# A fused attention, feed-forward and routed-expert kernel: weights converted in pairs, three step tables, smaller fixed expert capacities

## Chip, cores, metric

One core of a Trainium2 chip. The time is the device time of one execution in microseconds (us); the median of the runs is quoted. All inputs are in DRAM at the start, the output is in DRAM at the end.

## What is computed

Three layers in a row, cut from the reference:

```python
scores = scale * np.matmul(q, k.transpose(0, 1, 3, 2))        # B, H, S, D = 4, 8, 576, 64
kth = np.partition(scores, -32, axis=-1)[..., -32:-31]
scores = np.where(scores >= kth, scores, -1e9)                # the 32 largest of a row stay
x = (softmax(scores) @ v)  ->  [2304, 512]
h = x @ w_in; g = h * np.clip(h + 3, 0, 6) / 6; x = g @ w_out # w_in 512x2048, w_out 2048x512, float64
expert_idx = np.argmax(xn @ en.T / tau, axis=1)               # 8 second experts, one of them per token
out[mask] = gate_w[mask, None] * (np.maximum(x[mask] @ w1[e], 0) @ w2[e])   # w1 512x1024, w2 1024x512
```

`w_in` and `w_out` come as float64 and are taken apart on the chip; `w1` and `w2` are float32. Every float32 product is made of three TensorE products of a high and a low part (fp32r).

## The kernel before

**The step loop.** The attention is cut into 72 units (a head pair by 128 queries). `step(i)` runs in a loop of 76 steps and issues, for unit i and the four before it, one short operation after the other: scores (`score`), copies from PSUM (`take`), the selection of the 32 largest on VectorE (`pairs`, L409 to L413, and `pick0` to `pick3`, L428 and L431), the bounds on GpSimd (`bounds`, L436), relu and exp on ScalarE (`bend`, `expo`), a subtraction on GpSimd (`mask`, L446), transposes (`turn`, `keep`) and the product with v (`values`). From step 12 on a step also issues one eighth of a group of 256 tokens of the feed-forward layer (`s10`, `s11`, `gate`, `swish`, `large`, `small`, `s20`, `s21`). The order inside a step is a string of names: `FIRST` in steps 0 to 20, `THEN` afterwards. The engines run their own instructions in just that order, so each engine's queue is written out by hand here.

**Taking the weights apart.** In steps 0 to 18 the steps also convert `w_in` and `w_out`: 32 pairs of pieces of 128 x 256 values, one pair a step in steps 0 to 4 and two from step 5 on. A piece of float64 arrives as two int32 words each. VectorE makes the float32 bits of it with two scalar_tensor_tensor instructions (`w_one`, L234; `w_two`, L238), each over 128 x 256 and each with two tensors in SBUF. For three pieces of four ScalarE makes the rounding (`w_round`, L246) and GpSimd adds it (`w_add`, L251); for the fourth VectorE adds the next bits instead (L241). `w_hi` (ScalarE, L259) and `w_low` (GpSimd, L263) then split a pair into high and low part, and the low part goes to DRAM (`lo_dram`).

**After the loop** the rest of the feed-forward layer is issued through a scheduler (`whole`), eight parts per group. Each group of 128 tokens is routed: transposes, a product with the expert embeddings, `choose` (five small VectorE instructions), `rank` (two products and four small VectorE instructions) and `place` (an indirect DMA on GpSimd that writes a token's number into a table in DRAM). The last two groups are treated apart, in a part with an order written out (`tc.manual_schedule`): their transposes and routing stand between pieces of `stage1(0, 0, 256, ...)`, the first product of the first expert, and `split2(0, ...)` (ScalarE copy and VectorE subtraction of that expert's `w2`, L806 and L807) comes after `rank`.

**The second experts** are taken in the order of their token counts. Expert of rank r works on a fixed number `CAPS[r]` of tokens, gathered with indirect DMAs in blocks of up to 128 (`tokens`, L822, L826). `stage1` is 96 matmuls with `CAPS[r]` columns (L964), `stage2` 24 matmuls of 512 columns per block (L977). Rank 5 has a second bound: a conditional block behind all others (`tc.If(more > 0)`) takes tokens 256 to 383 when there are any. A block for whatever is above the capacities (`over_`) stands behind that.

Of the kernel before, what the change touches and what calls it, by code (L numbers as in the profile page):

```python
# [54 lines left out]
def fused_kernel(tc: tile.TileContext, *args):  # L55
# [35 lines left out]
def layers(tc: tile.TileContext, qt, kt, v, w_in, w_out, embt, tau, w1, w2, out, y_dram, g_dram, x_dram, tbl, lo_dram, flag, pools, consts):  # L91
# [4 lines left out]
    m1, sm, fs, ps_a = pools[1:]  # L96
# [15 lines left out]
    ordi = const.tile([1, 2 * E + 2], I32, name="ordi")  # L112
# [10 lines left out]
    stg = st.enter_context(tc.tile_pool(name="stg", bufs=5))  # L123
# [24 lines left out]
    def embed(part):  # L148
# [6 lines left out]
        elif part == 1:  # L155
            onesf = mp.tile([128, 128], F32, tag="ug", name="onesf", bufs=1)
            nc.vector.memset(onesf, 1.0)
            sq = fs.tile([128, 4, E], F32, tag="gts", name="sq")
            nc.vector.tensor_tensor(sq, emb["et"], emb["et"], op=ALU.mult)
# [3 lines left out]
        elif part == 2:  # L163
# [45 lines left out]
    def w_load(n):  # L209
        raws = []  # L210
        for src, dst in (wpieces[2 * n], wpieces[2 * n + 1]):
            single = src.dtype == F32
            if single:
                raw = stg.tile([128, 256], F32, tag="st", name="w32")
                nc.sync.dma_start(out=raw, in_=src)
            else:
                raw = stg.tile([128, 256, 2], I32, tag="st", name="w64")
                nc.sync.dma_start(out=raw, in_=src.bitcast(I32).rearrange("p (n two) -> p n two", two=2))
                cnt[0] += 1
            raws.append((raw, single, cnt[0] % 4 != 3))  # L220
        ent_[n] = dict(dst=wpieces[2 * n][1], raws=raws)

    def words_of(e):
        return [(raw, e["both"][:, 256 * o:256 * o + 256].bitcast(I32), rounded)
                for o, (raw, single, rounded) in enumerate(e["raws"]) if not single]

    def w_one(n):
        e = ent_[n]
        e["both"] = mp.tile([128, DM], F32, tag="wf", name="wf", bufs=3)
        for o, (raw, single, _) in enumerate(e["raws"]):  # L230
            if single:
                nc.vector.tensor_copy(e["both"][:, 256 * o:256 * o + 256], raw)
        for raw, t, _ in words_of(e):
            nc.vector.scalar_tensor_tensor(t, raw[:, :, 1], 3, raw[:, :, 1], op0=ALU.logical_shift_left, op1=ALU.bitwise_xor)  # L234

    def w_two(n):
        for raw, t, _ in words_of(ent_[n]):
            nc.vector.scalar_tensor_tensor(t, t, 0x3FFFFFFF, raw[:, :, 1], op0=ALU.bitwise_and, op1=ALU.bitwise_xor)  # L238
        for raw, t, rounded in words_of(ent_[n]):
            if not rounded:  # L240
                nc.vector.scalar_tensor_tensor(t, raw[:, :, 0], 29, t, op0=ALU.logical_shift_right, op1=ALU.bitwise_or)  # L241

    def w_round(n):
        for raw, single, rounded in ent_[n]["raws"]:
            if rounded and not single:
                nc.scalar.activation(raw[:, :, 0], raw[:, :, 0].bitcast(U32), AF.Copy, scale=2.0 ** -29)  # L246

    def w_add(n):
        for raw, t, rounded in words_of(ent_[n]):
            if rounded:  # L250
# [919 lines left out]
```

## Time and profile before

| | |
|---|---|
| median of 3 runs | 1165.76 us (1165.2 to 1168.55) |
| the profiled execution | 1164.9 us, its span 1163.2 us |
| busy, share of the span | TensorE 87%, weight loads 77%, VectorE 70%, ScalarE 63%, GpSimd 56% |
| mean granted TensorE clock | 0.937 |

Busy shares are means over stages with different limits, so the kernel is read by stretches: the step loop with the conversion (0 to about 241 us), the step loop without it (to about 748 us), the rest of the feed-forward layer (to about 885 us) and the second experts. A row of the view by lines gives source line, engine, operation, tiles and shape, then the group's busy time, the mean duration of one in ns, and the idle time of the engine before them with what ended it.

### The profile page before, as it was taken

To read this page: it belongs to the slowest core of one execution; us is meant where nothing else is said; L and a number is where in the kernel's file an instruction comes from. 1 tells how busy PE (TensorE), PEld (TensorE's weight loads), DVE (VectorE), ACT (ScalarE), POOL (GpSimd) and SP (SyncE) were. 2 spreads that over 40 slices of the span, in tenths; PEclk is the share of its full clock that TensorE was granted. 3 is DMA by queue.
4 is the path that set the end of the run, shared out by engine and by line. 5 is a ranking of instruction groups with operands and counts; after the bars stand their busy time and mean duration, and the time that the engine had idled before them with its cause. 6 is when DMAs were issued, how large, how long until landed. Compare 5 with 4: busy or idle time off the path is not lost. (4 is left out here: it accounts for less than half of the span.)

```text
span 1163.2 us, 21146 instructions
## 1 busy us (share of the span) xinstructions
PE 1008.5 (87%) x7200; PEld 892.1 (77%) x7200; DVE 818.5 (70%) x2429; ACT 732.6 (63%) x1486; POOL 646.4 (56%) x833
## 2 busy tenths in 40 slices
PE   2455576789999979999979998999989999999994
PEld 1344465679998869998868997889978788888884
DVE  4999999999788968788968789922142534444440
ACT  4676776878778868778868778743334444444540
POOL 5676776777666867666867666653231442213210
PEclk9966577889999989999989999999999999999998
DMA  6444455665443446443446244356765463344440
GB/s 179 146 137 138 164 167 174 185 199 204 123 123 116 134 144 194 123 123 118 136 121 213 82 146 128 110 128 177 235 214 208 117 221 122 128 175 148 173 175 20
DMA packets 93014, 176.45 MB, mean 152 GB/s; under 512 B 21135, under 2 KB 38690, under 8 KB 92895
## 3 DMA queue, kind: packets, MB, share of 16 engines
q1 hardware_dynamic: 88255, 164.90, 45.2%
q0 software_dynamic: 4640, 10.10, 2.6%
q8 instruction: 59, 0.97, 0.4%
q14 instruction: 60, 0.49, 0.1%
HBM read 151.15 MB, written 19.71 MB: 147 GB/s over the span
## 5 line engine op out<-in xcount | busy, mean ns | idle before, releaser
L446 POOL TENSOR_TENSOR s<-s,z 128x576 f32<-128x576 f32 x144 | 189.8, 1323 | 70.2 <-ACT z L442 69.5
L568 PE MATMUL bank_h<-xh,vh 128*128 128x256 f32 x576 | 177.0, 307 | 0.8 <-DVE u L580 0.8
L568 PE MATMUL bank_h<-xh,lo 128*128 128x256 f32 x576 | 167.7, 291 | 3.7 <-DMA lo<-lo_dram 3.7
L568 PE MATMUL bank_h<-xl,vh 128*128 128x256 f32 x576 | 167.7, 291 | 2.8 <-DVE xl L524 2.8
L428 DVE MAX8 A<-left 128x8 f32<-128x288 f32 (+1 forms) x288 | 159.7, 595 | 0.0
L397 PE MATMUL ps_sc<-kst,qh 128*128 128x288 f32 x256 | 90.8, 367 | 71.6 <-DVE left L413 35.9
L587 POOL TENSOR_TENSOR gl<-u,gh 128x512 fp32r<-128x512 f32 x72 | 93.2, 1295 | 102.8 <-ACT gh L584 88.8
L484 ACT COPY pt<-bank_t 128x384 f32<-128x384 f32 x216 | 100.4, 475 | 59.1 <-PE bank_t L479 58.9
L479 PE MATMUL bank_t<-ident,s 128*128 128x128 f32 x648 | 108.2, 294 | 28.0 <-ACT pt L484 16.7
L397 PEld LDWEIGHTS ps_sc<-kst,qh 128*128 128x128 f32 x256 | 55.7, 218 | 88.4 <-issue 73.6
L400 ACT COPY s<-ps_sc 128x576 f32<-128x576 f32 x144 | 91.5, 635 | 41.8 <-PE ps_sc L397 38.4
L568 PEld LDWEIGHTS bank_h<-xh,lo 128*128 128x128 f32 x576 | 114.2, 198 | 4.3 <-DMA lo<-lo_dram 4.3
L568 PEld LDWEIGHTS bank_h<-xl,vh 128*128 128x128 f32 x576 | 114.3, 198 | 3.6 <-DVE xl L524 3.1
L580 DVE SCALAR_TENSOR_TENSOR u<-u,bank_h 128x512 f32<-128x512 f32 x72 | 49.2, 684 | 95.6 <-ACT u L576 95.3
L603 PE MATMUL y<-wh,gh 128*128 128x512 f32 x288 | 116.3, 404 | 0.0
L807 DVE TENSOR_TENSOR l<-a,h 128x1024 fp32r<-128x1024 f32 x64 | 78.0, 1243 | 54.2 <-ACT h L806 51.5
L479 PEld LDWEIGHTS bank_t<-ident,s 128*128 128x128 f32 x648 | 82.3, 150 | 44.0 <-ACT pt L484 20.1
L568 PEld LDWEIGHTS bank_h<-xh,vh 128*128 128x128 f32 x576 | 114.2, 198 | 1.6 <-DVE u L580 1.0
L603 PE MATMUL y<-wh,gl 128*128 128x512 f32 x288 | 113.0, 397 | 2.0 <-POOL gl L587 2.0
L603 PE MATMUL y<-lo,gh 128*128 128x512 f32 x288 | 113.9, 396 | 0.2 <-DMA lo<-lo_dram 0.2
L442 ACT ACTIVATE z<-s,nb 128x576 bf16<-128x576 f32 x144 | 111.7, 780 | 0.8 <-POOL nb L436 0.7
L452 ACT ACTIVATE s<-s,nb 128x576 f32<-128x576 f32 x144 | 112.1, 778 | 0.0
(240 smaller groups left out, 2778.9 us busy)
## 6 DMA issues: line engine op xcount, KB each, us to landing
lo<-lo_dram SPq DMA_DIRECT2D x144, 512.0 KB, 4.2
a<-in_moe_w_dram SPq DMA_DIRECT2D x64, 512.0 KB, 7.4
qraw<-in_q_dram SPq DMA_DIRECT2D x64, 128.0 KB, 3.0
w<-in_moe_w_in_dram SPq DMA_DIRECT2D x32, 256.0 KB, 3.4
lo_dram<-wf SPq DMA_DIRECT2D x32, 256.0 KB, 2.4
w<-in_moe_w_out_dram SPq DMA_DIRECT2D x32, 256.0 KB, 3.0
vt<-in_v_dram SPq DMA_DIRECT2D x16, 320.0 KB, 4.5
kraw<-in_k_dram SPq DMA_DIRECT2D x32, 144.0 KB, 4.3
```

Of the source, the lines that this page charges most:

```text
L397: nc.tensor.matmul(ps[:, n, :HS], t, kk[:, HS * g:HS * g + HS], start=(o == 0), stop=(o == len(parts) - 1))
L400: nc.scalar.copy(sbuf[i % NS][:, :, HS * g:HS * g + HS], ps_[i][:, :, :HS])
L428: nc.vector.max(A[:, n, 8 * r:8 * r + 8], src[:, n, :w])
L442: nc.scalar.activation(zb_[n], tile_of(i, n), AF.Relu, bias=sel[i][1][:, n, 1:2], scale=-BIG)
L446: nc.gpsimd.tensor_tensor(s, s, zb_[n], op=ALU.subtract)
L452: nc.scalar.activation(s, s, AF.Exp, bias=sel[i][1][:, n, 0:1], scale=SCALE, accum_out=sums[i][:, n:n + 1])
L479: nc.tensor.transpose(pp[:, 128 * k:128 * k + 128], e[:, 128 * (3 * c + k):128 * (3 * c + k) + 128], ident)
L484: nc.scalar.copy(pts[i][:, 3 * c:3 * c + 3, :].rearrange("p k n -> p (k n)"), tb_.pop((i, c))[:, :384])
L568: nc.tensor.matmul(ph[:, a, :], w, x[:, k, :], start=(k == 0 and n == 0), stop=(k == 3 and n == 2))
L587: nc.gpsimd.tensor_tensor(state[q][1], state.pop((q, "u")).rearrange("p (a n) -> p a n", a=2), state[q][0].bitcast(F32), op=ALU.subtract)
L603: nc.tensor.matmul(state["y"][o], x[:, a, c], w, start=(f == 0 and n == 0), stop=(f == 15 and n == 2))
L807: nc.vector.tensor_tensor(lo, x, hi.bitcast(F32), op=ALU.subtract)
```

## The change

- `w_load` reads a whole pair with one DMA into one tile of 128 x 512 double words, three of them in turn instead of five half as wide. `w_one` becomes one tensor_scalar over 128 x 512 (shift and mask with constants), `w_two` one scalar_tensor_tensor over 128 x 512, `w_round` and `w_add` one instruction each over 128 x 512, for all pairs; the instruction of L241 is no longer used.
- Three tables: `FIRST` in steps 0 to 11, `MID` in steps 12 to 20, `THEN` afterwards, all with new orders (they are left out below; the pieces that the prediction speaks of are shown as instructions).
- `embed`, which prepares the expert embeddings, goes in five parts instead of four; its squares move from VectorE to ScalarE and its matmul to the step after them.
- `CAPS` falls by 32 for ranks 1, 2 and 3 and by 48 for rank 4; the conditional block of rank 5 goes.
- The part with the order written out for the last two groups goes. They are routed like all others, and the scheduler places `stage1(0, 0, 256)` and `split2(0)`. The weights of the second expert are asked for after the tables of all experts, and the value of its number is loaded there too.

```diff
-CAPS = (480, 384, 352, 336, 304, 256, 256, 240)
+CAPS = (480, 352, 320, 304, 256, 256, 256, 240)
-LAST, MOST = 5, 384
...
     def w_one(n):
         e = ent_[n]
+        raw = e["raw"]
         e["both"] = mp.tile([128, DM], F32, tag="wf", name="wf", bufs=3)
...
-        for raw, t, _ in words_of(e):
-            nc.vector.scalar_tensor_tensor(t, raw[:, :, 1], 3, raw[:, :, 1], op0=ALU.logical_shift_left, op1=ALU.bitwise_xor)
+        nc.vector.tensor_scalar(t, raw[:, :, 1], 3, 0x3FFFFFFF, op0=ALU.logical_shift_left, op1=ALU.bitwise_and)
     def w_two(n):
-        for raw, t, _ in words_of(ent_[n]):
-            nc.vector.scalar_tensor_tensor(t, t, 0x3FFFFFFF, raw[:, :, 1], op0=ALU.bitwise_and, op1=ALU.bitwise_xor)
-        for raw, t, rounded in words_of(ent_[n]):
-            if not rounded:
-                nc.vector.scalar_tensor_tensor(t, raw[:, :, 0], 29, t, op0=ALU.logical_shift_right, op1=ALU.bitwise_or)
+        nc.vector.scalar_tensor_tensor(t, raw[:, :, 1], -0x40000000, t, op0=ALU.bitwise_and, op1=ALU.bitwise_or)
...
-        for name in (FIRST if i < WORDS else THEN).split():
+        for name in (FIRST if i < MOES else MID if i < WORDS else THEN).split():
...
-        with tc.manual_schedule():
-            for o in range(2):
-                last[6](last[0], o)
-            st.close()
...
-            load1(1)
...
-            choose()
...
-            rank()
-            stage1(0, 0, 256, (4,))
-            split2(0, range(5, 8), lambda f: stage1(0, 0, 256, (f,)))
+        with tc.high_priority(offset=500):
+            stage1(0, 0, 256)
+        split2(0)
...
-        more = nc.values_load(ordi[0:1, 2 * E + 1:2 * E + 2], min_val=0, max_val=NT)
-        with tc.If(more > 0):
```

VectorE in step 6, before: the first of the step's two pairs (`w_642` and `w_644` are its two pieces).

```order
L234 SCALAR_TENSOR_TENSOR wf<-w_642 128x256
L234 SCALAR_TENSOR_TENSOR wf<-w_644 128x256
L428 MAX A<-top 128x8 x2
L431 MATCH_REPLACE top<-A,top 128x144 x2
L238 SCALAR_TENSOR_TENSOR wf<-wf,w_642 128x256
L238 SCALAR_TENSOR_TENSOR wf<-wf,w_644 128x256
L241 SCALAR_TENSOR_TENSOR wf<-w_642,wf 128x256
L428 MAX A<-top 128x8 x2
L431 MATCH_REPLACE left<-A,top 128x144 x2
L459 RECIPROCAL sums<-sums 128x2
L428 MAX A<-left 128x8 x2
L431 MATCH_REPLACE left<-A,left 128x288 x2
```

The same step now, with both pairs (`w_604`, `w_606`).

```order
L428 MAX A<-top 128x8 x2
L431 MATCH_REPLACE left<-A,top 128x144 x2
L231 TENSOR_SCALAR wf<-w_604 128x512
L238 SCALAR_TENSOR_TENSOR wf<-w_604,wf 128x512
L459 RECIPROCAL sums<-sums 128x2
L428 MAX A<-left 128x8 x2
L431 MATCH_REPLACE left<-A,left 128x288 x2
L428 MAX A<-left 128x8 x2
L231 TENSOR_SCALAR wf<-w_606 128x512
L238 SCALAR_TENSOR_TENSOR wf<-w_606,wf 128x512
L524 TENSOR_TENSOR xl<-bank_a,xh 128x128
```

Five VectorE instructions for that pair (four for the step's other one) have become two per pair, twice as wide.

VectorE behind the feed-forward layer, before: the end of `choose` and all of `rank` for the last two groups (`picks` is the choice, `rows` the place in the table); `hl` belongs to `stage1`, `l` to `split2`.

```order
L671 TENSOR_REDUCE first<-eqs 128x2
L672 TENSOR_TENSOR picks<-eqs,first 128x16
L967 SCALAR_TENSOR_TENSOR hl<-ph_10580,hh 128x256
L967 SCALAR_TENSOR_TENSOR hl<-ph_10595,hh 128x256
L684 TENSOR_TENSOR pos<-bank_a,ebase 128x16
L685 TENSOR_TENSOR pos<-pos,picks 128x16
L687 TENSOR_REDUCE de<-pos 128x2
L688 CAST rows<-de 128x2
L1038 TENSOR_TENSOR df<-l_all,mxs 128x144
L967 SCALAR_TENSOR_TENSOR hl<-ph_10618,hh 128x256
L759 COPY cnt_10692<-bank_a 1x8
L807 TENSOR_TENSOR l_10634<-a_10211,h_10633 128x1024
```

The same piece now.

```order
L665 TENSOR_REDUCE first<-eqs 128x2
L797 TENSOR_TENSOR l_10482<-a_10032,h_10481 128x1024
L666 TENSOR_TENSOR picks<-eqs,first 128x16
L797 TENSOR_TENSOR l_10482<-a_10032,h_10481 128x1024 x3
L966 SCALAR_TENSOR_TENSOR hl<-ph_10451,hh 128x256
L966 SCALAR_TENSOR_TENSOR hl<-ph_10466,hh 128x256
L678 TENSOR_TENSOR pos<-bank_a,ebase 128x16
L679 TENSOR_TENSOR pos<-pos,picks 128x16
L681 TENSOR_REDUCE de<-pos 128x2
L682 CAST rows<-de 128x2
```

The four wide subtractions of `split2` stand ahead of `rank` now, one of them inside `choose`. On TensorE, between the last product with the embeddings and the first transposes of expert 0's remaining tokens, there stood 72 matmuls of `stage1` (256 columns) and 31 of `stage2`; now there stand 24 and 48.

## Rows read from the trace of the kernel before

**Rows 1.** Stretches by engine: length, then busy us of PE, PEld, DVE, ACT, POOL; clock, DMA share, GB/s.
```profile
25.80:80.80 55.00, 26.79 (x133) 20.90 (x133) 54.62 (x164) 37.86 (x81) 38.10 (x47) 0.87 0.46 146
80.80:157.30 76.50, 45.30 (x274) 37.71 (x274) 76.30 (x218) 54.86 (x120) 55.83 (x67) 0.60 0.46 152
157.30:241.00 83.70, 58.42 (x408) 50.95 (x409) 81.84 (x220) 63.59 (x134) 60.70 (x71) 0.82 0.59 184
345.40:695.00 349.60, 331.75 (x2701) 298.61 (x2700) 295.41 (x1025) 269.26 (x579) 249.20 (x344) 0.97 0.46 137
915.00:1148.00 233.00, 229.58 (x1334) 200.68 (x1332) 104.38 (x139) 101.86 (x160) 60.52 (x59) 1.00 0.42 149
```

**Rows 2.** The same for the instructions of L234 alone (VectorE): busy us and count.
```profile
25.80:80.80 55.00, 6.28 (x14) 0.87 0.46 146
80.80:157.30 76.50, 8.96 (x24) 0.60 0.46 152
157.30:241.00 83.70, 14.26 (x22) 0.82 0.59 184
```

**Rows 3.** View by lines: the conversion's instructions on VectorE.
```profile
L234 DVE SCALAR_TENSOR_TENSOR wf<-w 128x256 int32<-128x256 int32 x64 | 32.2, 538 | 13.7 <-DMA w<-in_moe_w_in_dram 13.3 <-DMA w<-in_moe_w_out_dram 0.2
L238 DVE SCALAR_TENSOR_TENSOR wf<-wf,w 128x256 int32<-128x256 int32 x64 | 43.8, 723 | 0.0
L241 DVE SCALAR_TENSOR_TENSOR wf<-w,wf 128x256 int32<-128x256 int32 x16 | 18.5, 1157 | 0.0
```

**Rows 4.** One line's instructions (L238): shortest, median and longest duration in ns.
```profile
L238 DVE SCALAR_TENSOR_TENSOR wf<-wf,w x64: 407/520/1507, 15.0 to 233.6; 128x256 int32<-128x256 int32 x64
```

**Rows 5.** Timeline in step 10, VectorE and GpSimd: start us, duration us, instruction.
```profile
122.83 1.94 DVE L238 SCALAR_TENSOR_TENSOR wf<-wf,w 128x256 int32<-128x256 int32 x2
123.02 2.88 POOL L446 TENSOR_TENSOR s<-s,z 128x576 f32<-128x576 f32 x2
```

**Rows 6.** View by lines: instructions over 512 elements, and the rounding's addition.
```profile
L580 DVE SCALAR_TENSOR_TENSOR u<-u,bank_h 128x512 f32<-128x512 f32 x72 | 49.2, 684 | 95.6 <-ACT u L576 95.3
L587 POOL TENSOR_TENSOR gl<-u,gh 128x512 fp32r<-128x512 f32 x72 | 93.2, 1295 | 102.8 <-ACT gh L584 88.8 <-issue 9.0 <-POOL viol L438 3.3
L251 POOL TENSOR_TENSOR wf<-wf,w 128x256 int32<-128x256 int32 x48 | 38.5, 814 | 42.2 <-issue 20.1 <-DVE wf L238 8.7 <-DMA w<-in_moe_w_in_dram 6.7
```

**Rows 7.** View by lines: matmuls of `stage1` with 384 and 256 columns.
```profile
L964 PE MATMUL ph<-xl__11016,h 128*128 128x384 f32 x32 | 10.8, 339 | 0.3 <-DVE xl__11016 L828 0.3
L964 PE MATMUL ph<-xl__12092,h 128*128 128x256 f32 x32 | 9.0, 282 | 0.0
```

**Rows 8.** Timeline of TensorE in `stage2`: matmuls one behind the other.
```profile
951.66 0.39 PE L977 MATMUL po<-h,hl 128*128 128x512 f32 x1
951.89 0.40 PE L977 MATMUL po<-l,hh 128*128 128x512 f32 x1
```

**Rows 9.** Timeline: from the last groups' logits to expert 0's remaining tokens, several engines.
```profile
893.34 0.17 DVE L1016 COPY l_all<-bank_a 128x8 f32<-128x8 f32 x1 [1.21 <-PE bank_a L1015]
894.37 0.18 DVE L672 TENSOR_TENSOR picks<-eqs,first 128x16 bf16<-128x16 f32 x1
895.29 0.42 DVE L967 SCALAR_TENSOR_TENSOR hl<-ph,hh 128x256 fp32r<-128x256 f32 x1 [0.74 <-ACT hh L966]
...
897.66 0.17 DVE L688 CAST rows<-de 128x2 int32<-128x2 f32 x1
...
898.12 1.00 POOL L699 DMA_INDIRECT tbl<-ids,rows  x1 [3.02 <-DVE df L1038]
...
902.81 4.72 SPq L788 DMA_DIRECT2D idt<-tbl  x8
...
910.40 0.63 PE L826 MATMUL pxt<-ident,xg 128*128 128x128 f32 x4 [0.87 <-DMA xg<-y_dram,idt]
```

**Rows 10.** View by lines: the subtractions of the expert weights' splits.
```profile
L807 DVE TENSOR_TENSOR l<-a,h 128x1024 fp32r<-128x1024 f32 x64 | 78.0, 1243 | 54.2 <-ACT h L806 51.5 <-PE ph L964 1.9
```

**Rows 11.** Timeline: the end of the work, last write of the output.
```profile
1149.70 0.98 POOL L984 DMA_INDIRECT out_dram<-ob,idt  x1 [0.32 <-issue]
```

More of the change, by code (lines that the diff above doesn't have):

```diff
@@ L221, in w_load @@
[L221 to L225, printed above, removed]
+        src, dst = wpairs[n]
+        single = src.dtype == F32
+        if single:
+            raw = stg.tile([128, 2, 256], F32, tag="st", name="w32")
+            nc.sync.dma_start(out=raw, in_=src)
+        else:
+            raw = stg.tile([128, 512, 2], I32, tag="st", name="w64")
+            nc.sync.dma_start(out=raw.rearrange("p (a n) two -> p a n two", a=2), in_=src.bitcast(I32).rearrange("p a (n two) -> p a n two", two=2))
@@ L243, in w_round @@
     def w_round(n):
[L244 to L246 removed]
+        e = ent_[n]
+        if e["rounded"] and not e["single"]:
+            raw = e["raw"]
+            nc.scalar.activation(raw[:, :, 0], raw[:, :, 0].bitcast(U32), AF.Copy, scale=2.0 ** -29)
     def w_add(n):
[L249 to L251 removed]
+        e = ent_[n]
@@ L253, in parts_of @@
+        if e["rounded"] and not e["single"]:
+            nc.gpsimd.tensor_tensor(e["words"], e["words"], e["raw"][:, :, 0], op=ALU.add)
     def parts_of(e):
@@ L844, in ahead @@
         load2(0)
-        expert(1)
     def step(i, last):
@@ L921, in layers @@
         rest = True
-        while moe or side:
+        while moe or last or side:
             if not rest and "order" in late and "w1" not in late:
@@ L939, in layers, with split2 @@
                 finish_rest()
-        assert "w1" in late and done_groups[0] == NG - 2
+        if "w1" not in late:
+            at.close()
+            ahead()
+        assert done_groups[0] == NG and "order" in late
+        st.close()
+        hp = mb.enter_context(tc.tile_pool(name="hp", bufs=1))
+        tk = mb.enter_context(tc.tile_pool(name="tk", bufs=1))
+        wb = mb.enter_context(tc.tile_pool(name="wb", bufs=1))
+        gp = mb.enter_context(tc.tile_pool(name="gp", bufs=3))
+        px = mb.enter_context(tc.tile_pool(name="px", bufs=2, space=PSUM))
+        po_ = mb.enter_context(tc.tile_pool(name="po_", bufs=3, space=PSUM))
         hs = {}
-        def split2(r, then=(), f=None):
-            then = deque(then)
+        def split2(r):
             a2 = ws2[r]
@@ L948, in split2, with stage1 @@
                 split(h2[:, k:k + 2, :], l2[:, k:k + 2, :], a2[:, k:k + 2, :])
-                if then:
-                    f(then.popleft())
             ws2[r] = (h2, l2)
-        def stage1(r, c0, c1, fs_=range(8)):
+        def stage1(r, c0, c1):
             xh_, xl_ = tok[r]
@@ L958, in stage1 @@
             hh, hl = hs[r]
-            for f in fs_:
+            for f in range(8):
                 ph = late["ph"].tile([128, 512], F32, tag="ph", name="ph2")[:, :c1 - c0]
@@ L1070, in layers @@
                 split2(then)
-        more = nc.values_load(ordi[0:1, 2 * E + 1:2 * E + 2], min_val=0, max_val=NT)
-        with tc.If(more > 0):
-            for c in range(CAPS[LAST], MOST, 128):
-                tokens(LAST, [(c // 128, c, 128)], pps)
-                stage1(LAST, c, c + 128)
-                stage2(LAST, [(c // 128, c, 128)])
         mb.close()
```

134 lines of the change are left out of this document (49 added, 85 removed).

## The prediction, made before the changed kernel was run

> **What bounds the kernel now.** I read the busy times by stretch first [rows 1]. From 25.8 to 241 us, the steps that convert weights, VectorE is busy 54.62 of 55.00, 76.30 of 76.50 and 81.84 of 83.70 us: 98 to 100%. No other engine passes 76% there, so these 215 us are VectorE's. From 345 to 695 us TensorE is busy 331.75 of 349.60 us (95%) and VectorE 84%; from 915 to 1148 us TensorE has 229.58 of 233.00 us (99%). So a saving on VectorE counts in full up to about 241 us, as far as the next engine allows, and nothing behind it; a saving of matmuls counts in full in the second experts. What is saved early stays saved, since the later stretches are TensorE's own work.
>
> The profiled execution took 1164.9 us, 0.86 us under the median of 1165.76; the sum is made against it. About 0.3% (3.5 us) is what a measurement of this kernel can tell from no change.
>
> **Term 1, the conversion on VectorE.** Now it costs 32.2 + 43.8 + 18.5 = 94.5 us [rows 3], over 32 pairs 2.95 us each. One of these instructions takes 407 ns at best [rows 4]; 144 of them would take 59 us, so 36 us, 0.25 us per instruction, is waiting inside them. Rows 5 show for what: two L238 take 1.94 us while GpSimd runs two subtractions of L446.
>
> The Trainium skill (SBUF — State Buffer, "Who interferes with whom") says that a VectorE instruction with two inputs in SBUF and a GpSimd instruction that reads SBUF exclude each other for the whole instruction. The trace agrees: 407 ns alone, up to 1507 ns beside GpSimd [rows 4].
>
> A pair now has two instructions over 512 elements. The trace has no integer one of that size. The nearest row of the kind is L580, scalar_tensor_tensor over 512 elements, 684 ns [rows 6]; I take it for both and add the same wait of 0.25 us to each: 2 x 0.934 = 1.87 us. The lower bound is no wait and a tensor_scalar as short as today's 256-element instruction: 0.41 + 0.68 = 1.09 us. The upper bound is that double width costs double, waits too: (32.2 + 43.8) / 32 = 2.38 us, so that only L241's share is gained.
>
> The skill (VectorE: DVE Perf Modes, "The perf-mode tier table") lets a float32 tensor_scalar in SBUF run two elements a cycle; were that so here, an estimate from that page's cycle table is 0.33 us in place of 0.68, and the sum would come out some 11 us lower. No row here shows it, and the sum doesn't use it.
>
> The three stretches hold 14, 24 and 22 instructions of L234 [rows 2], so 7, 12 and 11 pairs. VectorE's work in them becomes 54.62 - 7 x 1.08 = 47.1, 76.30 - 12 x 1.08 = 63.3 and 81.84 - 11 x 1.08 = 70.0 us. ScalarE has 37.9, 54.9 and 63.6 us, GpSimd 38.1, 55.8 and 60.7 [rows 1]. On GpSimd three additions of 0.81 us a step become two of about 1.30 (L587 has that size) [rows 6]: 0.2 us more a step. ScalarE's roundings, three half as wide against two, move by less. So VectorE stays the longest, but only 10 to 15% ahead, and three engines that feed each other don't reach 100%. I take the 95% that the longest engine of the later steps reaches [rows 1]: 49.5, 66.7 and 73.6 us. **Gain 5.5 + 9.8 + 10.1 = 25 us**, plus 1 us for the two pairs outside these stretches, of which the first hides behind its load: **26 us**.
>
> Bounds. With 1.09 us per pair VectorE falls to 41.6, 54.0 and 61.4 us; GpSimd's 55.8 + 1.2 us and ScalarE's 63.6 bound then, and at 95% the stretches are 43.8, 60.0 and 66.9 us: gain 44 us. With 2.38 us they are 53.3, 73.1 and 79.6 us: gain 9 us.
>
> **Edits that go with it, costed at nothing.** The DMAs of a pair become one instead of two, the same bytes; VectorE waits 13.7 us for them in all [rows 3], nearly all of it ahead of 25.8 us, since it is busy 98 to 100% from there on. Three wide buffers hold three pairs, five narrow ones two and a half. If a load came late, ScalarE's rounding would wait and GpSimd's addition with it. The embedding's matmul goes to a step of its own; VectorE's queue bounds there today, so its present wait costs nothing. The new `THEN` order works where TensorE is busy 95% [rows 1]: nothing, and 5 us either way in the range.
>
> **Term 2, the capacities.** 32 + 32 + 32 + 48 = 144 columns fewer, each in 96 matmuls. Between 384 and 256 columns a matmul differs by 339 - 282 = 57 ns [rows 7], 0.445 ns a column: 144 x 96 x 0.445 ns = 6.2 us. Rank 4 falls to 256 and loses its third block: 24 matmuls of 512 columns, one each 0.23 us [rows 8]: 5.5 us. TensorE is busy 99% there, so both count: **11.5 us**. The weights' loads lie beside it at a DMA share of 0.42 [rows 1]; rank 4's stretch shrinks by 7 us of TensorE work, and the load of the next weights would be late next.
>
> The conditional block does nothing but load a number and branch. The last write waits 0.32 us for nothing but its issue [rows 11]; that is the most the branch can cost on the path, and I leave it out.
>
> **Term 3, the hand-over to the second experts.** Before, from the last logits to the first transposes of expert 0's remaining tokens, 893.34 to 910.40 us, the chain is: choice, rank, table written, numbers read back, gather [rows 9]. That is 17.1 us, and TensorE filled it but for 0.87 us, with 72 and 31 matmuls. In the new order four subtractions of `split2`, 1.24 us each [rows 10], stand ahead of the rank's VectorE instructions, where before only two short ones of `stage1` stood. The choice comes 1.2 us later, at 895.8; three more of 1.24 us, two short ones of 0.42 us and four small ones of 0.2 follow: rows ready at about 901.1 instead of 897.8, so the table's writes, the reading back on SP and the gathers, all queued behind it, come 3.3 us later: 20.4 us. TensorE has 48 matmuls of 0.23 us, 24 of half the columns and 1 us of small products in that time: 14.8 us. It would idle 5.6 us instead of 0.9: **loss 5 us**. SP asks for the second expert's weights only behind the reading back, at about 911 us by the same clock; 2 MB need some 12 us more at the 149 to 184 GB/s of rows 1, and TensorE still has 96 matmuls of 224 columns and some 40 of 512 of expert 0, about 19 us. Bounds: 0, if ScalarE and VectorE get ahead; 12 us, if the last loads and splits come late too.
>
> **Sum.** 1164.9 - 26 - 11.5 + 5 = 1132.4 for a profiled execution; with the 0.86 us of the median **1133 us**.
>
> **Rivals.**
> 1. *The steps fall to the next engine without waits.* 44 + 11.5 us gained, no loss at the hand-over: 1110 us. For it: ScalarE and GpSimd are at 69 to 76% in these stretches now [rows 1]. Against: GpSimd's queue is mostly instructions that exclude those of VectorE. Chance 0.2.
> 2. *Only the fourth piece's instruction is gained, or the steps go over to ScalarE's and GpSimd's queues at once.* 9 us in the loop, 12 us lost at the hand-over: 1157 us. For it: in step 10 each VectorE instruction of the conversion meets a GpSimd one [rows 5]. Chance 0.2.
> 3. *Slower: the lock between VectorE and GpSimd.* If every instruction of the conversion waited a whole GpSimd instruction (1.10 us, rows 4), a pair would cost 2 x 1.78 = 3.57 us, 0.62 us more than now; over 30 pairs 18.6 us. With 11.5 us gained and 5 to 12 lost: 1178 to 1185 us. It decides from a mean wait of 0.9 us per instruction on, against 0.25 now; the place is steps 1 to 18. The skill's page on SBUF says that a tensor_scalar can also take the shared ports. No run here shows it. Chance 0.05.
> 4. *The capacities are too small and the spare block runs.* From the reference's inputs the counts by rank are 475, 339, 299, 288, 232, 231, 215, 225, all at or under the new capacities, with 13 or more to spare in the changed ranks. Chance 0.01.
>
> **How the numbers follow.** Forecast (about 1118 to 1148) 0.52, rival 1 0.2, rival 2 0.2, rivals 3 and 4 0.06, no change 0.02. The range of 8 in 10 takes in most of rivals 1 and 2: **1111 to 1154 us**. Faster by over 0.3% 0.91, within 0.3% 0.03, slower 0.06.
>
> **What would show it.** In the changed profile: VectorE's group of L231 and L238 (32 each) near 60 us in all, against 94.5; the converting steps ended near 215 us instead of 241; GpSimd over 76% in the converting steps; TensorE idle 5 to 6 us ahead of the transposes of L816; no third block of rank 4. The prediction is wrong if VectorE isn't the longest in the first 230 us, if the conversion's wait per instruction is far from 0.25 us, or if TensorE's idle time behind 250 us grows by more than 10 us.

## The result, and the profile after

The changed kernel takes **1114.34 us** (median of 4 runs, 1112.74 to 1116.48) against 1165.8 us: ratio **0.9555, interval 0.9532 to 0.9579**. Forecast were 1133 us, 1111 to 1154 us. The time lies inside the range, 19 us under the point, and that gap is not one error in size: one term of the sum was missing. The profiled execution took 1116.48 us, its span is 1114.8 us (before 1163.2).

A step begins in VectorE's queue with L409, once a step; the starts of this line give the time by part. Shortest, median and longest of it in ns, then the first and last start in us, before and after:

```profile
L409 DVE TENSOR_TENSOR ps_sc<-ps_sc,s x72: 435/456/467, 15.7 to 748.2; 128x288 f32<-128x288 f32 x72
```

```profile
L409 DVE TENSOR_TENSOR ps_sc<-ps_sc,s x72: 439/449/467, 15.4 to 701.6; 128x288 f32<-128x288 f32 x72
```

| begins at, us | before | after | gained up to here |
|---|---|---|---|
| step 6 | 80.8 | 71.6 | 9.2 |
| step 12 | 157.3 | 135.2 | 22.1 |
| step 18 | 241.0 | 214.8 | 26.2 |
| step 19 | 250.6 | 223.5 | 27.1 |
| step 71 | 748.2 | 701.6 | 46.6 |
| end of the span | 1163.2 | 1114.8 | 48.4 |

So 27.1 us come from the converting steps (forecast 26), 19.5 us from steps 19 to 71 (forecast 0) and 1.8 us from all behind them (forecast 6.5, from 11.5 less 5).

The stretches of the changed kernel by engine, columns as in [rows 1]:

```profile
24.20:71.60 47.40, 25.95 (x133) 19.61 (x133) 46.88 (x148) 38.99 (x78) 37.03 (x44) 0.89 0.52 159
71.60:135.20 63.60, 41.64 (x278) 33.12 (x279) 61.65 (x187) 56.22 (x118) 57.94 (x60) 0.73 0.57 186
135.20:214.80 79.60, 56.77 (x399) 48.75 (x398) 67.38 (x190) 62.90 (x126) 62.18 (x67) 0.83 0.61 189
223.50:701.60 478.10, 467.49 (x3909) 416.41 (x3905) 424.04 (x1482) 384.45 (x835) 355.81 (x501) 1.00 0.46 144
```

VectorE is busy 99, 97 and 85% of the converting stretches: it still bounds the first two; in the third it is the longest too, but stands idle for 12 us. GpSimd is at 78, 91 and 78%.

The conversion in the view by lines, which answers to [rows 3]:

```profile
L238 DVE SCALAR_TENSOR_TENSOR wf<-w,wf 128x512 int32<-128x512 int32 x32 | 29.1, 908 | 0.9
L231 DVE TENSOR_SCALAR wf<-w 128x512 int32<-128x512 int32 x32 | 23.2, 726 | 19.8 <-DMA w<-in_moe_w_in_dram 13.2 <-DMA lo_dram<-wf 6.6
...
L251 POOL TENSOR_TENSOR wf<-wf,w 128x512 int32<-128x512 int32 x32 | 41.4, 1293 | 21.3 <-ACT s L400 5.2 <-POOL viol L438 4.1 <-PE ps_sc L397 2.5
```

and shortest, median and longest of the two VectorE lines in ns, as in [rows 4]:

```profile
L231 DVE TENSOR_SCALAR wf<-w x32: 409/553/1443, 14.2 to 207.1; 128x512 int32<-128x512 int32 x32
...
L238 DVE SCALAR_TENSOR_TENSOR wf<-w,wf x32: 691/694/1659, 14.6 to 207.7; 128x512 int32<-128x512 int32 x32
```

94.5 us have become 23.2 + 29.1 = 52.3 us, 1.63 us a pair (forecast 1.87, about 60 us in all). The tensor_scalar takes 409 ns at best, the scalar_tensor_tensor of the same width 691 ns. The Trainium skill (VectorE: DVE Perf Modes, "The perf-mode tier table") gives tensor_scalar with float32 in SBUF twice the rate of a one-element-a-cycle instruction; the trace agrees in direction, for int32 words, short of the 0.33 us estimated from that page.

**Where the 19.5 us came from.** Before, steps 35 to 37 and 53 to 55, counted by their L409 as in the table, were slow. The three steps from 35 on and the three from 53 on, before:

```profile
399.60:434.10 34.50, 28.05 (x203) 24.92 (x201) 25.69 (x90) 23.81 (x50) 24.36 (x36) 0.85 0.50 137
573.90:608.60 34.70, 27.44 (x202) 24.41 (x201) 25.54 (x89) 23.66 (x50) 24.13 (x36) 0.85 0.47 130
```

The same steps after:

```profile
373.70:400.70 27.00, 24.35 (x196) 20.78 (x196) 24.73 (x89) 21.68 (x46) 25.15 (x32) 1.00 0.68 199
540.00:565.40 25.40, 23.82 (x196) 20.88 (x196) 24.62 (x89) 21.73 (x46) 24.15 (x31) 1.00 0.73 200
```

7.5 + 9.3 = 16.8 us of the 19.5 lie in these six steps. Before, no engine was busy over 82% in them, though TensorE's mean over [rows 1]'s 350 us was 95%. The timeline of ScalarE at the place, before (start, duration, idle time ahead and what ended it):

```profile
407.08 0.41 ACT L373 CAST qh<-qraw 128x256 fp32r<-128x256 f32 x1
410.00 0.67 ACT L322 CAST kst<-kraw 128x576 fp32r<-128x576 f32 x1 [2.51 <-DMA kraw<-in_k_dram]
...
412.45 0.45 ACT L484 COPY pt<-bank_t 128x384 f32<-128x384 f32 x1
```

and of TensorE:

```profile
409.70 0.28 PE L568 MATMUL bank_h<-xl,vh 128*128 128x256 f32 x1
409.82 0.28 PE L568 MATMUL bank_h<-xh,lo 128*128 128x256 f32 x1
412.95 0.90 PE L479 MATMUL bank_t<-ident,s 128*128 128x128 f32 x3 [2.86 <-ACT pt L484]
...
413.87 0.42 PE L568 MATMUL bank_h<-xl,vh 128*128 128x256 f32 x1
414.08 0.41 PE L568 MATMUL bank_h<-xh,lo 128*128 128x256 f32 x1
```

ScalarE stands at its copy of k (L322, in `prep`) until the load of k has landed; the copies of `pt` are queued behind it, and TensorE's transposes wait for those. After TensorE's 2.86 us of idling its matmuls follow each other at 0.21 us instead of 0.12 us: the granted clock is 0.50 of full speed there, the lower of its two levels (1.2 GHz against 2.4 GHz), as the seventh number of this stretch shows:

```profile
412.90:417.00 4.10, 4.04 (x19) 4.05 (x19) 1.93 (x10) 2.73 (x6) 3.76 (x5) 0.50 0.01 2
```

The idle time ahead of L322, first before, then after:

```profile
L322 ACT CAST kst<-kraw x16: 667/672/685, 5.1 to 599.0; 128x576 fp32r<-128x576 f32 x16
...
  DMA kraw<-in_k_dram: 18.8, 8
```

```profile
L322 ACT CAST kst<-kraw x16: 666/673/712, 5.0 to 556.9; 128x576 fp32r<-128x576 f32 x16
...
  DMA kraw<-in_k_dram: 8.0, 9
```

**What stopped the third converting stretch.** After, the embedding's product (L166) and what stands behind it:

```profile
150.82 0.28 DVE L524 TENSOR_TENSOR xl<-bank_a,xh 128x128 fp32r<-128x128 f32 x1
...
151.25 1.85 PE L166 MATMUL bank_a<-sq,onesf 128*128 128x8 f32 x8 [8.85 <-DVE xl L524]
...
158.42 0.69 ACT L576 ACTIVATE u<-bank_h,half 128x512 f32<-128x512 f32 x1 [9.03 <-PE bank_h L568]
...
159.14 0.69 DVE L580 SCALAR_TENSOR_TENSOR u<-u,bank_h 128x512 f32<-128x512 f32 x1 [5.03 <-ACT u L576]
```

TensorE stands 8.85 us until VectorE has read the bank, the feed-forward matmuls come late, ScalarE with them, and VectorE idles 5.03 us. Before, the same product was as late, and VectorE had enough work queued not to notice (0.70 us):

```profile
186.74 1.45 PE L162 MATMUL bank_a<-sq,onesf 128*128 128x8 f32 x6 [9.29 <-DVE sq L159]
...
191.01 0.17 DVE L459 RECIPROCAL sums<-sums 128x2 f32<-128x2 f32 x1 [0.70 <-POOL sums L456]
```

**The hand-over.** After, the transposes of expert 0's remaining tokens (before: 0.87 us in [rows 9]):

```profile
874.30 1.11 PE L816 MATMUL pxt<-ident,xg 128*128 128x128 f32 x4 [5.44 <-DMA xg<-y_dram,idt]
877.36 0.90 PE L816 MATMUL pxt<-ident,xg 96*128 96x96 f32 x4 [1.94 <-DMA xg<-y_dram,idt]
```

### The profile page after: what moved, and what is told of

The parts are those of the page before. It is cut to its first block, busy times and chain, and to the rows that moved or that the text cites. A ratio compares the mean times of both kernels' runs of the same rounds, so it can differ in the third digit from the quotient of the medians.

```text
span 1114.8 us, 20782 instructions
## 1 busy us (share of the span) xinstructions
PE 983.8 (88%) x7172; PEld 861.7 (77%) x7172; DVE 775.3 (70%) x2345; ACT 727.1 (65%) x1469; POOL 646.6 (58%) x815
## 4 chain that ended last, share of the span: by engine, by line
PE 66%; DVE 12%; issue 7%; DMA 6%; ACT 5%; POOL 2%; SPq 1%; POOLq 0%; DVEq 0%; ACTq 0%
PE bank_h L568 17%; PE y L603 15%; PE ph L963 8%; PE po L976 7%; PE bank_a L497 6%; PE ps_sc L397 5%; PE bank_t L479 5%; DVE A L428 3%; DVE left L431 2%; DMA xg<-y_dram,idt 1%; DMA a<-in_moe_w_dram 1%; PE bank_t L640 1%; DVE wf L238 1%; DVE wf L231 1%; DMA lo_dram<-wf 1%
## 5 line engine op out<-in xcount | busy, mean ns | idle before, releaser
L568 PE MATMUL bank_h<-xh,vh 128*128 128x256 f32 x576 | 170.7, 296 | 1.1 <-DVE u L580 1.1
L568 PE MATMUL bank_h<-xl,vh 128*128 128x256 f32 x576 | 164.5, 286 | 2.2 <-DVE xl L524 2.2
L568 PE MATMUL bank_h<-xh,lo 128*128 128x256 f32 x576 | 164.4, 285 | 0.0
L479 PE MATMUL bank_t<-ident,s 128*128 128x128 f32 x648 | 104.8, 288 | 35.9 <-ACT pt L484 30.9
L397 PE MATMUL ps_sc<-kst,qh 128*128 128x288 f32 x256 | 87.8, 356 | 44.9 <-DVE left L413 21.2
L479 PEld LDWEIGHTS bank_t<-ident,s 128*128 128x128 f32 x648 | 73.2, 145 | 54.0 <-ACT pt L484 36.0
L568 PEld LDWEIGHTS bank_h<-xh,lo 128*128 128x128 f32 x576 | 111.8, 194 | 0.1
L497 PE MATMUL bank_a<-pt,vt 128*64 128x128 f32 (+1 forms) x1600 | 107.6, 289 | 0.7 <-DVE pos L678 0.7
L497 PEld LDWEIGHTS bank_a<-pt,vt 128*64 128x64 f32 x1600 | 89.7, 152 | 23.3 <-issue 8.0
```

What stands on the lines that cost most here:

```text
L397: nc.tensor.matmul(ps[:, n, :HS], t, kk[:, HS * g:HS * g + HS], start=(o == 0), stop=(o == len(parts) - 1))
L479: nc.tensor.transpose(pp[:, 128 * k:128 * k + 128], e[:, 128 * (3 * c + k):128 * (3 * c + k) + 128], ident)
L497: nc.tensor.matmul(av[64 * n:64 * n + 64, c0:c1], vt[:, k, 64 * n:64 * n + 64], pt[:, k + 5 * n if k < 4 else 4, c0:c1], start=(o == 0), s ...
L568: nc.tensor.matmul(ph[:, a, :], w, x[:, k, :], start=(k == 0 and n == 0), stop=(k == 3 and n == 2))
```

## The experiments

These runs were made later, on three chips. The kernel before took about 1172 to 1174 us in them instead of 1165.8, so whole kernels are compared by their ratios to it; `after_again`, `early_loadk`, `both_tail` and `caps_only` share one chip. Steps and stretches are read from each run's profile. Medians and intervals:

| run | us | ratio | interval |
|---|---|---|---|
| `after_again` | 1118.42 | 0.9530 | 0.9500 to 0.9560 |
| `pairs_only` | 1145.51 | 0.9775 | 0.9734 to 0.9816 |
| `then_back` | 1148.84 | 0.9785 | 0.9725 to 0.9846 |
| `loadk_first` | 1159.86 | 0.9893 | 0.9851 to 0.9935 |
| `embed_early` | 1112.34 | 0.9478 | 0.9418 to 0.9537 |
| `embed_y` | 1108.82 | 0.9458 | 0.9415 to 0.9501 |
| `early_loadk` | 1108.94 | 0.9449 | 0.9417 to 0.9481 |
| `mid_store` | 1131.56 | 0.9645 | 0.9604 to 0.9686 |
| `caps_back` | 1129.61 | 0.9618 | 0.9550 to 0.9685 |
| `caps_only` | 1170.71 | 0.9976 | 0.9954 to 0.9997 |
| `tail_back` | 1122.69 | 0.9580 | 0.9518 to 0.9643 |
| `both_tail` | 1113.93 | 0.9498 | 0.9466 to 0.9530 |

> The changed kernel itself once more, on the same chip as the three below, as their measure. Every theory: the ratio that it had, 0.953 to 0.958; 1114 us if this chip is as fast as the first one, up to 1122 us if it is like the chip of the runs so far, on which the kernel before took 1174 us.

The ratio agrees with that of the first measurement, 0.9555, within the intervals.

**The conversion alone.** `pairs_only` is the kernel before with the new `w_load`, `w_one`, `w_two`, `w_round` and `w_add`; two buffers change with it for room:

```diff
-    stg = st.enter_context(tc.tile_pool(name="stg", bufs=5))
+    stg = st.enter_context(tc.tile_pool(name="stg", bufs=3))
...
-            yt = m1.tile([128, 4, 128], F32, tag="yt", name="yt")
+            yt = mp.tile([128, DM], F32, tag="ug", name="yt", bufs=1).rearrange("p (k n) -> p k n", k=4)
```

> The kernel before with the conversion by pairs alone (one DMA, tensor_scalar and scalar_tensor_tensor over 512 elements, three wide buffers); its own two tables, embedding, capacities and hand-over stay. Theory: the form of the instructions is the gain of the converting steps, so step 18 begins near 215 us instead of 241 and the whole is 25 to 28 us faster than before: ratio 0.976 to 0.979, about 1139 us. Rival: the new tables FIRST and MID carry half of it: step 18 near 228 us, ratio 0.987 to 0.99, about 1153 us.

Step 18 begins at 213.7 us, step 19 at 222.8 us: the whole gain of the converting steps. Its two VectorE lines:

```profile
L234 DVE SCALAR_TENSOR_TENSOR wf<-w,wf 128x512 int32<-128x512 int32 x32 | 31.7, 990 | 0.5
L227 DVE TENSOR_SCALAR wf<-w 128x512 int32<-128x512 int32 x32 | 27.0, 844 | 16.7 <-DMA w<-in_moe_w_in_dram 14.3 <-DMA lo_dram<-wf 1.5 <-DMA w<-in_moe_w_out_dram 0.8
```

58.7 us, 1.83 us a pair, near the 1.87 of the forecast. The changed kernel, which differs from this one up to step 19 in its tables `FIRST` and `MID` and in `embed`, comes down to 1.63 us a pair, and loses that again at the embedding.

**The order of the later steps.** `then_back` puts the old `THEN` into the changed kernel (its first words below); `loadk_first` moves one word in the kernel before (its first line below).

```diff
-THEN = ("lows turn0 pick0 expo0 keep0 turn1 expo1 s10 s11 ship bend0 turn2 score0 keep1 pick1 guard gate take0 keep2 inverse "
...
+THEN = ("pick0 turn0 turn1 expo0 keep0 s10 expo1 lows ship turn2 pick1 pick2 s11 keep1 keep2 guard bend0 score0 gate take0 load_k "
...
```

```diff
-THEN = ("pick0 turn0 turn1 expo0 keep0 s10 expo1 lows ship turn2 pick1 pick2 s11 keep1 keep2 guard bend0 score0 gate take0 load_k "
+THEN = ("load_k pick0 turn0 turn1 expo0 keep0 s10 expo1 lows ship turn2 pick1 pick2 s11 keep1 keep2 guard bend0 score0 gate take0 "
```

> The changed kernel with the table THEN of the kernel before; everything else stays. Theory: the new table is what shortens steps 19 to 71, by 19.5 us, since ScalarE no longer stands at the copies of k (L322) waiting for their load. Then this kernel is 17 to 20 us slower than the changed one: 1131 to 1135 us, with steps of 11 to 13 us back behind steps 35 and 53 and some 18 us of ScalarE idle before L322. Rival A: the gain is the phase that the faster conversion leaves, or the other buffers: within 3 us of 1114. Rival B: half and half, 1122 to 1126 us.

> The kernel before with one word moved in THEN: load_k, the load of the next k, stands first in a step instead of behind take0. Theory: what the new THEN gains is the time between the load of k and ScalarE's copy of it (L322), for which ScalarE stood 18.8 us in all. Then this alone takes the steps behind 35 and 53 back from 25 to 17 us each: 15 to 17 us faster than before, ratio 0.985 to 0.987, about 1149 us, and less than 5 us of idle time before L322. Rival: the load waits in SP's queue for the raw k's buffer, or ScalarE's wait only moves to another load: ratio 0.997 to 1.003, 1162 to 1169 us. Slower, if SP stands at that place and the loads of the low parts come late behind it: over 1169 us.

In `then_back` steps 19 to 71 take 498.6 us against 478.1: the 20 us are back, with the slow steps (those from 35 on):

```profile
374.50:410.40 35.90, 27.94 (x202) 24.86 (x201) 26.29 (x90) 23.57 (x50) 25.28 (x36) 0.86 0.52 142
```

and the idle time before L322 (us, times):

```profile
  DMA kraw<-in_k_dram: 21.0, 9
```

It is 30 us slower than the changed kernel by the ratios, where 17 to 20 were expected: some 10 us more lie behind the loop, which the table had no part in; that stays open (below). In `loadk_first` the six steps fall to 26.9 and 26.0 us:

```profile
400.70:427.60 26.90, 23.91 (x202) 21.18 (x201) 25.33 (x89) 21.80 (x48) 24.64 (x36) 1.00 0.59 173
567.50:593.50 26.00, 23.65 (x202) 21.16 (x201) 25.22 (x89) 21.95 (x48) 23.77 (x35) 1.00 0.59 172
```

and the idle time before L322 nearly goes:

```profile
  DMA kraw<-in_k_dram: 3.1, 3
```

Steps 19 to 71 take 482.8 us against 497.6: one word gives 14.8 of the 19.5 us. By the ratio the whole kernel gains 12.6 us, where 15 to 17 were expected. So most of the gain is the time between the load of k and ScalarE's copy of it, not the phase that the conversion leaves: `pairs_only`, with the new conversion and the old `THEN`, takes 501.7 us for these steps. The clock has a share in it: with nearly the same number of matmuls TensorE is busy 28.05 us (203) and 27.44 us (202) in the slow steps before, 23.91 and 23.65 us (202 each) in `loadk_first`. The other 5 us of the new order weren't taken apart.

**The embedding.** `embed_early` has its five parts at steps 0 to 4; `embed_y` has them at steps 8 to 12 and the product in another bank.

```diff
-        if i in (11, 12, 13, 14, 16):
-            embed((11, 12, 13, 14, 16).index(i))
+        if i in (0, 1, 2, 3, 4):
+            embed(i)
```

```diff
-            emb["pe"] = pe = half_a()
+            emb["pe"] = pe = ps_y.tile([128, DM], F32, tag="y", name="pe")
...
-        if i in (11, 12, 13, 14, 16):
-            embed((11, 12, 13, 14, 16).index(i))
+        if i in (8, 9, 10, 11, 12):
+            embed((8, 9, 10, 11, 12).index(i))
```

> The changed kernel with the five parts of the embedding's preparation at steps 0 to 4 instead of 11, 12, 13, 14 and 16. Theory: in the changed kernel TensorE stands 8.85 us before the embedding's product (L166, waiting for the subtraction L524 of the same step), and VectorE, which no longer covers it, then idles 5.03 us at L580. Without it 4 to 5 us faster: 1109 to 1110 us. Rival: the steps 12 to 18 are bound by the stores of the low parts (VectorE waits 5.2 us for them at L231), so the stall only moves: 1113 to 1115 us. Against both: the first steps are VectorE's (99% busy), and the embedding's VectorE work of some 2 us now lies there: up to 2 us less gain.

> The changed kernel with the embedding's five parts at steps 8 to 12, and its product in one of the two PSUM tiles that the feed-forward's output uses later, so that it waits for no subtraction of the step. Theory: the 5.03 us of VectorE at L580 go and nothing is added to the first steps (embed_early lost 4.6 us there): steps 12 to 18 take 72 us as in embed_early, step 18 begins near 208 us, and the whole is 6 to 7 us faster than the changed kernel, 1107 to 1109 us. Rival: the table loads on ScalarE (two of 1.28 us) and the embedding's VectorE work lie wherever they are put, and steps 12 to 18 are bound by the stores of the low parts: 1112 us, like embed_early.

In both, steps 12 to 18 shrink from 79.6 us to 72. `embed_early` pays 3 to 5 us for it in steps 0 to 5; `embed_y` doesn't and begins step 18 at 208.7 us, against 212.6 us; their ratios lie within the noise of each other. Its stretch from step 12 to 18:

```profile
136.90:208.70 71.80, 55.03 (x394) 45.98 (x393) 67.07 (x191) 60.02 (x122) 62.49 (x66) 0.88 0.68 210
```

and in the timeline the product, with nothing waited for:

```profile
110.08 0.95 PE L166 MATMUL pe<-sq,onesf 128*128 128x8 f32 x8
```

Against `after_again`, whose step 18 begins at 218.2 us, it begins that step 9.5 us earlier and gains some 8 us by the ratios, more than the 5.03 us of that one stall: in the changed kernel three more waits of VectorE, of 1.3 to 1.5 us, follow it in this stretch, and in `embed_y` they are gone too. That the embedding's work has only moved is ruled out: steps 6 to 12, where it lies now, take 64.3 us, in `after_again` 63.9. VectorE still isn't full in this stretch (93%): it waits at L231. `mid_store` was to take the waits for stores away in the changed kernel, by issuing `low1` and `store1` earlier:

```diff
-       "load_k store0 keep1 turn2 add0 hi1 swish one1 take0 mask0 keep2 load_q inverse score1 large values round1 two1 take1 "
-       "pick2 aside bend1 load0 scale xh pick3 low1 small add1 mask1 need_v pairs xl prep load1 store1 bounds")
+       "load_k store0 keep1 turn2 add0 hi1 swish one1 take0 mask0 low1 store1 keep2 load_q inverse score1 large values round1 two1 take1 "
+       "pick2 aside bend1 load0 scale xh pick3 small add1 mask1 need_v pairs xl prep load1 bounds")
```

> The changed kernel with low1 and store1 moved forward in MID, behind mask0, so that the second pair's low part is stored half a step earlier. Theory: VectorE's waits at L231 for these stores, 5.2 us in steps 12 to 18, fall to under 2 us: 3 to 4 us faster, 1110 to 1111 us. Rival: the stall at the embedding's product and ScalarE set these steps anyway: 1113 to 1116 us. Slower (over 1118 us) if GpSimd stands at low1 for ScalarE's rounding and the additions behind it come late.

It is slower, as its last case said, and the waits that it was to take away have not fallen: VectorE stands 6.5 us at L231 for stores in steps 12 to 18, against 5.2. GpSimd in these steps, first in the changed kernel, then in `mid_store`:

```profile
L263 POOL TENSOR_TENSOR wf<-wf,wh 128x512 fp32r<-128x512 f32 x6 | 8.3, 1388 | 3.2 <-ACT wh L259 3.2
L263 POOL TENSOR_TENSOR wf<-wf,vh 128x512 fp32r<-128x512 f32 x6 | 8.2, 1368 | 0.0
```

```profile
L263 POOL TENSOR_TENSOR wf<-wf,vh 128x512 fp32r<-128x512 f32 x6 | 8.2, 1370 | 7.4 <-ACT vh L259 7.4
L263 POOL TENSOR_TENSOR wf<-wf,wh 128x512 fp32r<-128x512 f32 x6 | 8.1, 1348 | 7.2 <-ACT wh L259 7.2
```

GpSimd stands 14.6 us for ScalarE's copy where it stood 3.2. Step 19 begins at 232.3 us, 5.8 us behind `after_again`; some 8 us more lie behind the loop (below).

`early_loadk` is `embed_y` with `load_k` at the head of the new `THEN`:

```diff
-THEN = ("lows turn0 pick0 expo0 keep0 turn1 expo1 s10 s11 ship bend0 turn2 score0 keep1 pick1 guard gate take0 keep2 inverse "
+THEN = ("load_k lows turn0 pick0 expo0 keep0 turn1 expo1 s10 s11 ship bend0 turn2 score0 keep1 pick1 guard gate take0 keep2 inverse "
...
-        "mask0 swish scale large aside bend1 pick2 load_k s20 pick3 score1 take1 s21 values small prep mask1 pairs place xh "
+        "mask0 swish scale large aside bend1 pick2 s20 pick3 score1 take1 s21 values small prep mask1 pairs place xh "
```

> The changed kernel with the embedding as in embed_y and load_k first in THEN. Theory: 6 us from the embedding's stall, as embed_y showed, and what is left of ScalarE's waiting at L322 (8.0 us in the changed kernel), of which most lies beside other work, so 1 to 3 us: 7 to 9 us faster than after_again. Rival: the new THEN already gives the load the time it needs, and SP's order gets worse by the move: equal to embed_y, 5 to 6 us faster than after_again.

The wait before L322 falls to 3.5 us, and the time is that of `embed_y`: what was left of it lay beside other work. These two beat both kernels: 1109 us; `early_loadk` lies 9.5 us under the changed one on the same chip.

**Capacities and hand-over.** `caps_back` is the changed kernel with the old `CAPS`, `caps_only` the kernel before with the new ones and no conditional block; `tail_back` is the changed kernel with the old hand-over, `both_tail` the same on top of `early_loadk`. For `caps_back` and `caps_only`:

```diff
-CAPS = (480, 352, 320, 304, 256, 256, 256, 240)
+CAPS = (480, 384, 352, 336, 304, 256, 256, 240)
```

```diff
-CAPS = (480, 384, 352, 336, 304, 256, 256, 240)
+CAPS = (480, 352, 320, 304, 256, 256, 256, 240)
...
-LAST, MOST = 5, 384
+LAST, MOST = 5, 256
...
-        more = nc.values_load(ordi[0:1, 2 * E + 1:2 * E + 2], min_val=0, max_val=NT)
-        with tc.If(more > 0):
...
```

For `tail_back` and `both_tail` the old lines of the hand-over are put back, in part:

```diff
-        late["wb"] = wb
+        with tc.manual_schedule():
+            for o in range(2):
+                last[6](last[0], o)
...
+            load1(1)
...
+            rank()
+            stage1(0, 0, 256, (4,))
+            split2(0, range(5, 8), lambda f: stage1(0, 0, 256, (f,)))
         with tc.high_priority(offset=500):
-            stage1(0, 0, 256)
-        split2(0)
...
```

> The changed kernel with the eight capacities of the kernel before (no conditional block). Theory, as in term 2 of the prediction: 144 columns in 96 matmuls and 24 matmuls of 512 columns more, 6.2 + 5.5 = 11.5 us: 1126 us. Rival: the loads and splits of the next weights bind in the second experts, so the matmuls saved were given back as waiting: 5 us or less, at most 1119 us.

> The kernel before with the new capacities and without the conditional block, nothing else. Theory of term 2: 11.5 us faster than before, ratio 0.990. Rival: the gathers and loads that the matmuls covered come late (3.28 us at one gather in tail_back), so 6 to 8 us: ratio 0.993 to 0.995. The stretch from the last step of the loop to the end was 414.9 us before: 403 us by the theory, 407 to 409 us by the rival.

> The changed kernel with the hand-over of the kernel before (the order written out for the last two groups, the second expert's weights asked for early); capacities as changed, no conditional block. Theory, as in term 3: TensorE's 5.4 us of idling before the transposes of L816 fall to about 1, so 5 us faster: 1109 us. A larger value, 8 us (1106 us), if the short waits behind 700 us also go (gaps above 0.25 us there sum to 19.6 us against 11.6 before). Rival: no gain, 1114 us, since TensorE only waits at another place, for the loads of the weights.

> early_loadk with the hand-over of the kernel before. Theory of term 3: 4 to 5 us faster than early_loadk. Rival, from tail_back, in which TensorE's idling before the transposes of L816 fell from 5.44 to 1.12 us but came back as 3.28 and 1.61 us at the gathers of later experts: 0 to 2 us faster.

TensorE's work from step 71 to the end, `caps_back` first, then the changed kernel:

```profile
705.10:1127.70 422.60, 389.78 (x2412) 343.13 (x2410) 157.57 (x286) 167.96 (x283) 118.61 (x120) 0.97 0.48 156
```

```profile
701.60:1114.70 413.10, 378.32 (x2384) 332.57 (x2382) 157.33 (x285) 165.60 (x281) 113.81 (x117) 0.97 0.48 159
```

11.46 us of matmuls, as costed. By the ratios `caps_back` is some 10 us slower than the changed kernel (0.9618 against 0.9530). But beside the old hand-over the same capacities bring 0.24% (0.03 to 0.46%), some 3 us, in `caps_only`, where 11.5 us by the theory or 6 to 8 by the rival were expected. And the old hand-over does shorten the wait at expert 0's tokens, `tail_back`:

```profile
869.36 0.63 PE L827 MATMUL pxt<-ident,xg 128*128 128x128 f32 x4 [1.12 <-DMA xg<-y_dram,idt]
```

yet it is no faster: 0.958 against 0.953, and `both_tail` is 5 us above `early_loadk`, on the same chip. The part from step 71 to the end in the profiles (the span less step 71's start), us:

| hand-over | old capacities | new capacities |
|---|---|---|
| old | 415.0 (the kernel before), 419.1 (`pairs_only`), 424.5 (`loadk_first`) | 411.3 (`caps_only`), 412.7 (`tail_back`), 414.9 (`both_tail`) |
| new | 422.7 (`caps_back`) | 410.5 to 413.3 in five runs, but 423.3 and 421.5 in `then_back` and `mid_store` |

So the same code behind the loop differs by up to 13 us from one profile to another, and the table can't price the hand-over: with the new capacities both lie at 410 to 415 us, those two runs aside. Between the first two profiles, before and after, all changes behind step 71 together show 1.8 us; against the other two runs with the old code there they show 6 to 11 us. The profiled executions of `caps_only`, `tail_back` and `both_tail` were the fastest of theirs, 3 to 8 us under the medians; where those microseconds lie in the other executions isn't known.

What happens to the matmuls saved beside the old hand-over can be seen in `caps_only`. TensorE from step 71 on, the kernel before first:

```profile
748.20:1163.10 414.90, 387.52 (x2415) 342.17 (x2413) 159.48 (x286) 168.63 (x280) 117.55 (x122) 0.98 0.49 160
```

```profile
749.80:1161.00 411.20, 378.79 (x2386) 332.87 (x2385) 156.78 (x285) 165.22 (x278) 114.08 (x119) 0.97 0.49 160
```

8.7 us less work, 3.7 us less time. At the tokens of a later expert:

```profile
979.86 1.93 SPq L793 DMA_DIRECT2D a<-in_moe_w_dram  x4
980.90 0.96 POOL L822 DMA_INDIRECT xg<-y_dram,idt  x1 [0.30 <-issue]
...
988.98 0.63 PE L826 MATMUL pxt<-ident,xg 128*128 128x128 f32 x4 [3.70 <-DMA xg<-y_dram,idt]
```

A gather issued among the weights' loads takes 8 us to the transposes, and TensorE, with fewer matmuls to do, waits for it; 2.31 us more go at the next expert. `both_tail` has 3.05 us at that place. In the changed kernel's profile TensorE waits 0.90 us there; in `then_back` and `mid_store`, with the same code behind the loop, it waits 3.64 and 3.54 us. What decides which of the two comes about wasn't settled.

## Why the prediction was right, and where it was wrong

**What bounds.** VectorE up to 241 us: right, and it is still the longest in all three stretches, though in the third it stands idle for 15% of the time. From 345 to 695 us the forecast went by TensorE's mean and saw nothing else to gain there: wrong, as `THEN` below shows.

**Term 1.** 26 us forecast, 27.1 measured, 27.8 by `pairs_only`: right in total, and its mechanism is shown by that run. Its parts were off both ways: VectorE reaches 97 to 99% in the first two stretches where 95% was taken, and a pair costs 1.63 us instead of 1.87 (1.83 with the old tables); so steps 0 to 6 and 6 to 12 gave 9.2 and 12.9 us instead of 6.5 and 9.8, and the third stretch 4.1 instead of 10.1. That they cancel in the total is luck. Inside a pair the wait was right (0.32 and 0.22 us an instruction for 0.25); the tensor_scalar's own time was not, 409 ns where 684 were taken.

**The embedding at nothing.** This is the step that failed in the third stretch: "VectorE's queue bounds there today, so its present wait costs nothing". The cover named was the very queue that the change shortens. Its 8.85 us wait left 5.03 us of VectorE idle; taken away, with the shorter waits behind it, the kernel is some 8 us faster (`embed_y`).

**`THEN` at nothing.** The step that failed most, by 19.5 us: "works where TensorE is busy 95% [rows 1]: nothing, and 5 us either way in the range". The 95% is a mean over some 35 steps; six of them cost 17 us too much and had TensorE at 80%. Behind its idle time there stood ScalarE's wait for the load of k. The sequence of step lengths, 8 to 11 us with 11.6, 13.5, 12.2 and 13.2 among them, was in the trace and would have shown it.

**Term 2.** The size of the work was right (11.46 us for 11.5), "so both count" was not: beside the new hand-over some 10 us came of it, beside the old one 3 us, and from step 71 on the first two profiles differ by 1.8 us in all.

**Term 3.** The wait came as costed (5.44 us for 5.6, and 1.94 more). That it is a loss did not hold: with the old hand-over and the new capacities the kernel is no faster, by `both_tail` slower, and waits of the same size stand at later experts there (3.28 and 1.61 us in `tail_back`). The two terms should have been priced together.

**The sum.** Forecast -26 - 11.5 + 5 = -32.5 us, measured -48.4 in the profiles: -27.1 - 19.5 - 1.8. Rival 1 named the nearer number, 1110 us, for a reason that did not occur: 44 us in the conversion. Rival 2, with 9 us in the loop, fell at 27.1 us. Rival 3 fell: a wide instruction's mean is 0.73 and 0.91 us, 0.32 and 0.22 us above its shortest, far from the 0.9 us of waiting that would have made the kernel slower. No spare block ran (rival 4).

## What to carry to other kernels

A new order inside a loop is not priced by an engine's mean share over the loop: list the length of every step, and ask of the longest steps which wait ended last. A stall that "the bound engine covers" has to be held against that engine's queue as the change leaves it. And matmuls saved ahead of a gather can come back as waiting for it: 8.7 us less work gave 3.7 us less time in the profile of `caps_only`.

## What the runs showed that was not expected

- On this VectorE a tensor_scalar over 128x512 int32, read with a stride of two words, takes 409 ns at best, a scalar_tensor_tensor of the same size 691 ns. Over 128x256 the latter took 407 ns at best [rows 4], so twice the width cost 1.7 times as much.
- The tensor_scalar, with one tensor in SBUF alone, is held up by GpSimd too: in the changed kernel it took 420 to 427 ns in the four cases in which GpSimd ran nothing beside it, and 1.02 to 1.05 us in the six that began inside one of GpSimd's additions of L251.
- A gather that was issued behind two of the weights' loads took 8 us to the transposes (`caps_only`).
- After 2.86 us of idling TensorE's matmuls of 256 columns followed each other at 0.21 us instead of 0.12 us; the six slow steps lost to the lower level of the clock (granted 0.85 over them, 1.00 in the changed kernel and in `loadk_first`) as well as to the waits: some 4 us of TensorE's busy time at each of the two places.
